# A decode-attention kernel: the output weights loaded once in long rows, in-place adds, and no Block

## The chip, the cores and the metric

One core of one Trainium2 chip. Times are device microseconds of one execution, quoted as the median of several. A profile also has a span, from the first to the last instruction of the profiled execution. In a profile PE is TensorE (its matmuls; PEld its weight loads), DVE is VectorE, ACT ScalarE, POOL GpSimd and SP SyncE; a packet is one record of the DMA in the trace, in these loads one contiguous row (64 loads of 128 rows of 32 KB have 8,192 packets of 32 KB). Executions of one kernel mostly agree within 0.3% (the kernel before: 662.87 to 664.14 us in four, 0.2%), so a difference of one or two microseconds in 663 is at the edge of what can be told.

## The reference

Attention of one new token against a cache, then a gated feed-forward layer, for a batch of 2:

```python
# B=2, D=512, 32 heads of Dh=128, cache length Sk=8192, F=1376, all bf16
q = (layernorm(x) @ wq)                       # per head
p = softmax(q . k_cache * Dh**-0.5)
o = p . v_cache                               # [B, 32*128]
h = x + o @ wo                                # wo: [4096, 512]
l = layernorm(h)
out = h + (relu(l @ W_gate) * (l @ W_up)) @ W_down
```

The two caches are 268 MB of the 281 MB that must be read. There is very little arithmetic per byte.

## The kernel before

A "pair" is two heads of one batch element; there are 32 pairs. The K and V of a pair are 128 rows of 32 KB each, one row in each SBUF partition, and four slots of 4 MB hold them:

```python
def kv(cache, p):
    hp, b = divmod(p, B)
    return cache[b, 2 * hp:2 * hp + 2].rearrange("h (p j) d -> (h p) (j d)", p=64)

with nc.Block() as block:
    @block.sync
    def _(eng):
        def load(s, cache, p):
            nc.sync.dma_start(slot[s][:], kv(cache, p)).then_inc(slot_sem[s], 16)
        def load_wo(dst, g, sem):      # two heads: 128 rows of 2 KB
            nc.sync.dma_start(
                dst[:], A_wo[2 * g * Dh:2 * (g + 1) * Dh].rearrange("(p r) n -> p (r n)", r=2)).then_inc(sem, 16)
        ...
        # cut: PE loop over two pairs: transposes and scores of K, collect, p.V, o_proj with wo_cur
        # cut: VectorE's share of the scores, for each pair p
        dve: prod = k_t[:, 0:jd, :] * q                     # L474
        cur, w, tog = prod[:, 0:jd, :], Dh, 0
        while w > 8:                                        # halving adds, L482
            half = w // 2
            o = tb[...] if tog == 0 else prod[:, 0:jd, 0:half]
            nc.vector.tensor_tensor(out=o, in0=cur[:, :, 0:half], in1=cur[:, :, half:w], op=ALU.add)
            cur, w, tog = o, half, tog ^ 1
        ...
        if p % 2 == 1 and 1 <= g < NI:
            load_wo(wo_cur, g, sem_wo)                      # every two pairs
        ...
        elif p == NP - 3:                                   # the last V, in two halves by columns
            for k, (j0, j1) in enumerate(((J // 2, J), (0, J // 2))):
                nc.sync.dma_start(slot[3][:, j0 * Dh:j1 * Dh],
                                  kv(A_v_cache, NP - 1)[:, j0 * Dh:j1 * Dh]).then_inc(sem_vl[k], 16)
```

`collect` sums the partial outputs of a pair of heads with 32 small float32 matmuls and `o_proj` multiplies the two finished heads by their rows of wo. After the last pair comes the tail: collection, projection, layer norm, the two up-projections, W_down, and the output.

The softmax here doesn't subtract the row's maximum and nothing guards it: scores larger than these inputs give would overflow.

Of the kernel before, what the change touches and what calls it, by code (L numbers as in the profile page):

```python
# [7 lines left out]
F32 = mybir.dt.float32  # L8
# [31 lines left out]
def bass_sequential_preLN__gqa_block_cached__glu_gated_reglu__decode_kernel(  # L40
# [26 lines left out]
    PG = 2  # L67
    NI = NP // 2 - 1
# [4 lines left out]
    with ExitStack() as es:  # L73
# [16 lines left out]
        sem_x, sem_wq, sem_wo, sem_wl, sem_out = S("x"), S("wq"), S("wo"), S("wl"), S("out")  # L90
# [5 lines left out]
        wo_cur = sb("wo_cur", [128, 2 * D], BF16)  # L96
# [3 lines left out]
        tb = sb("tb", [128, JC * 64], BF16)  # L100
# [9 lines left out]
        qrep = [tb[:, i * 512:(i + 1) * 512] for i in range(2)]  # L110
# [7 lines left out]
        NS = 4  # L118
        scores = [sb(f"scores{i}", [128, JC], F32) for i in range(NS)]
        e_t = [sb(f"e{i}", [128, J // VJ, 32], BF16) for i in range(PG)]  # L120
        zs = sb("zs", [128, 4, 2], F32)
        zr = sb("zr", [128, B], F32)
        zi = sb("zi", [128, B], F32)
        O_cur = sb("O_cur", [128, 2, B], BF16)
# [6 lines left out]
        h_r = sb("h_r", [128, 128], F32)  # L131
        o_r = sb("o_r", [128, 128], BF16)
# [5 lines left out]
        zero = sb("zero", [128, 8], BF16)  # L138
# [15 lines left out]
        with nc.Block() as block:  # L154

            @block.sync
            def _(eng):
# [4 lines left out]
                def load_wo(dst, g, sem):  # L162
                    nc.sync.dma_start(
                        dst[:], A_wo[2 * g * Dh:2 * (g + 1) * Dh].rearrange("(p r) n -> p (r n)", r=2)).then_inc(sem, 16)
# [5 lines left out]
                load_wo(wo_cur, 0, sem_wo)  # L170
                load_wo(wo_last, NI, sem_wl)
# [10 lines left out]
                for c in range(4):  # L182
                    pool.last()
                    pool.run(nc.gpsimd.tensor_copy(
                        out=sel[32 * c:32 * c + 32, :].rearrange("p (j a q) -> p j a q", j=VJ, q=PG),
                        in_=ident_f[32 * c:32 * c + 32, 32 * c:32 * c + 16].rearrange("p (q j a) -> p j a q", j=VJ, q=PG)))
# [3 lines left out]
                pool.run(nc.gpsimd.memset(zero[:], 0.0))  # L190
# [61 lines left out]
                dve.eng.memset(O_cur[:], 0.0).then_inc(d2p, 1)  # L252
                sp.wait(t_q)
                load(3, A_v_cache, 1)

# [25 lines left out]
                pe.wait(t_const, t_q2, t_q_b)  # L281
                pe.run(nc.tensor.matmul(Wp[:, 0:DC * B], lhsT=ident[:], rhs=zero[:], start=True, stop=False,
# [50 lines left out]
                def pv(T, p, parts):  # L333
# [4 lines left out]
                    for j0, j1, waits in parts:  # L338
                        for sem, val in waits:
                            nc.tensor.wait_ge(sem, val)  # L340
                        for j in range(j0, j1, VJ):
                            c = 32 * (n % 4)
                            i = nc.tensor.matmul(  # L343
                                Op[0][c:c + 32, :], lhsT=e_t[q][:, j // VJ, :],
                                rhs=v_t[:, j:j + VJ, :].rearrange("p j d -> p (j d)"),
                                start=(q == 0 and n < 4), stop=(q == PG - 1 and n >= J // VJ - 4))
                            n += 1
                    T.mark(("pv", p), i)

                def collect(T, a):  # L350
                    nc.tensor.wait_ge(a2p, a)
                    for r in range(2):
                        for jj in range(VJ):
                            for a_ in range(2):
                                i = nc.tensor.matmul(  # L355
                                    Ob[64 * a_:64 * a_ + 64, B * r:B * r + B],
                                    lhsT=os_sb[:].rearrange("p (j d r) -> p j r d", j=VJ, r=2)[:, jj, r, :],
                                    rhs=sel[:, (2 * jj + a_) * B:(2 * jj + a_) * B + B],
                                    start=(jj == 0), stop=(jj == VJ - 1))
                    T.mark("ob", i)  # L360

                def z_sum(T, bank):
                    for a in range(2):
                        i = nc.tensor.matmul(
                            bank[64 * a:64 * a + 64, ZC:ZC + 2 * B], lhsT=ones_f[:, 0:64],
                            rhs=zs[:].rearrange("p (b a) k -> p a b k", a=2)[:, a], start=True, stop=True)
                    T.mark("z", i)

                def o_proj(T, w, last=False):
                    wv = w[:].rearrange("p (r n c) -> p r c n", n=128, c=DC)  # L370
                    for r in range(2):
                        for c in range(DC):
                            i = nc.tensor.matmul(
                                Wp[:, c * B:(c + 1) * B], lhsT=wv[:, r, c, :], rhs=O_cur[:, r, :],
                                start=False, stop=last, skip_group_check=True)
                    T.mark("om", i)

                with nc.Fori(0, NI, engines=OrderedEngineSet([nc.tensor.engine])):
# [5 lines left out]
                    nc.tensor.wait_ge(d2p, 1)  # L384
                    nc.tensor.wait_ge(v2p, 2)
                    o_proj(body, wo_cur)
                    nc.tensor.sem_inc(d2p, -1)
                    pv(body, 1, ((jd, J, ((v2p, 3), (a2p, 12))), (0, jd, ((a2p, EV),))))
                    z_sum(body, Ob)
                    nc.tensor.sem_inc(g2p, -2)  # L390
                    nc.tensor.sem_inc(v2p, -3)
# [7 lines left out]
                k_part(tail, P0, 0, ((slot_sem[0], 256), (g2p, 1)))  # L399
                collect(tail, 6)  # L400
                ob_last_loop = tail.at["ob"]
                k_part(tail, P1, 7, ((slot_sem[2], 256), (g2p, 2)))
                nc.tensor.wait_ge(d2p, 1)
                nc.tensor.wait_ge(sem_wo, 16 * NI)
                o_proj(tail, wo_cur)
                pv(tail, P0, ((j30, J, ((slot_sem[1], 256), (a2p, 5))), (0, j30, ((a2p, 7),))))
                nc.tensor.wait_ge(a2p, 17)
                z_sum(tail, Op[1])
                pv(tail, P1, ((j31, J, ((sem_vl[0], 16), (a2p, 16))), (0, j31, ((sem_vl[1], 16), (a2p, 17)))))

# [25 lines left out]
                def normalize(bank, t_z):  # L436
                    dve.wait(t_z)
                    dve.run(nc.vector.tensor_reduce(  # L438
                        out=zr[:], in_=bank[:, ZC:ZC + 2 * B].rearrange("p (n k) -> p n k", k=2), axis=AX.X, op=ALU.add))
# [4 lines left out]
                def o_scale(t_ob):  # L444
                    dve.wait(t_ob)
                    nc.vector.tensor_tensor(
                        out=O_cur[:], in0=Ob[:, 0:2 * B].rearrange("p (r b) -> p r b", b=B),
                        in1=zi[:].unsqueeze(1).broadcast_to([128, 2, B]), op=ALU.mult).then_inc(d2p, 1)

                t_dm, t_s = {}, {}  # L450
                for p in range(NP):
# [12 lines left out]
                    if p < P0:  # L464
                        if p % 2 == 1:
                            nc.gpsimd.wait_ge(sem_wo, 16 * max(1, g))
                            nc.gpsimd.sem_inc(v2p, 1)
                        nc.gpsimd.wait_ge(slot_sem[s + 1], 16 * (g + 1))
                        nc.gpsimd.sem_inc(v2p, 1)

                    dve.wait((slot_sem[s], 16 * (g + 1)), t_q_b)
# [4 lines left out]
                    cur, w, tog = prod[:, 0:jd, :], Dh, 0  # L476
                    while w > 8:
                        half = w // 2
                        o = (tb[:, 0:jd * half].rearrange("p (j w) -> p j w", w=half) if tog == 0
                             else prod[:, 0:jd, 0:half])  # L480
                        dve.last()
                        dve.run(nc.vector.tensor_tensor(  # L482
                            out=o, in0=cur[:, :, 0:half], in1=cur[:, :, half:w], op=ALU.add))
                        cur, w, tog = o, half, tog ^ 1
                    dve.last()
                    sc = scores[p % NS]
                    t_s[p] = dve.run(nc.vector.tensor_reduce(out=sc[:, 0:jd], in_=cur, axis=AX.X, op=ALU.add))  # L487
                    if p % 2 == 0 and p >= 2:
                        t_ob = tok("ob", g) if g < NI else (pe.sem, ob_last_loop)
                        normalize(Ob, t_ob)  # L490
                        o_scale(t_ob)

                    for gg in range(ng):
                        act.wait(tokp("pt", p, gg))
                        if gg >= 2:
                            act.wait(tokp("sc", p, gg - 2))
                        elif p >= 1:
                            act.wait(tokp("sc", p - 1, NG - 2 + gg))
                        to_pe(nc.scalar.activation(  # L499
                            out=kT[gg % 2][:], in_=Tp[gg % 2][:].bitcast(BF16), func=ACT.Copy))  # L500
                    act.wait(tokp("sc", p, ng - 1), t_const)
                    exp(p, 0, lambda h, a: Sp[p % 2][h, 0:2 * ng * GT].rearrange(
                        "p (g j a) -> p g j a", a=2, j=VJ)[:, :, :, a])
                    if p % 2 == 0:
# [3 lines left out]
                    act.wait(t_s[p])  # L508
                    exp(p, 1, lambda h, a: sc[h, 0:jd].rearrange("p (g j) -> p g j", j=VJ))
# [4 lines left out]
                    if p % 2 == 1 and 1 <= g < NI:  # L514
                        sp.wait(tok("om", g))
                        load_wo(wo_cur, g, sem_wo)
# [11 lines left out]
                    elif p == NP - 2:  # L528
                        sp.wait(t_dm[p], tokp("pt", p, NG - 1))
                        for r0, r1 in ((0, 80), (80, 88), (88, FR)):  # L530
                            nc.sync.dma_start(
                                wd_last[r0:r1, :], B_W_down[F - FR + r0:F - FR + r1]).then_inc(sem_wd[3], 16)
# [148 lines left out]
```

## Time and profile before

| | before |
|---|---|
| time, median (range) of three executions | 663.05 us (662.87 to 664.14) |
| span of the profiled run | 661.1 us |
| bytes read, mean rate | 281 MB, 425 GB/s |
| third K load: last byte landed at | 64.7 us |
| last weight (W_down, third part): landed at | 657.8 us |

Landing times are the completion records that the trace has for each load: 16 of them for each of these loads, which I take as one from each DMA engine; "landed" means the last.

From the page of the kernel before: the span, the DMA rows of the 40 slices (busy tenths, and GB/s moved), the packet counts, the chain that ended last, and three groups of VectorE instructions.

```profile
span 661.1 us, 8515 instructions
...
DMA  9999999999999999999999999999999999999996
GB/s 381 429 426 439 421 438 429 434 424 430 438 430 428 428 430 440 427 431 428 428 438 430 428 430 430 437 427 428 429 434 432 432 424 432 436 419 442 430 419 276
DMA packets 12689, 281.22 MB, mean 425 GB/s; under 512 B 1442, under 2 KB 1540, under 8 KB 3972
...
DMA 71%; DVE 23%; PE 2%; POOL 2%; ACT 1%; issue 0%; SPq 0%; DVEq 0%; POOLq 0%
...
L474 DVE TENSOR_TENSOR prod<-slot,q_b 128x12288 bf16<-128x12288 bf16 (+1 forms) x32 | 207.7, 6491 | 128.9 <-DMA slot<-in_A_k_cache_dram 127.3
L482 DVE TENSOR_TENSOR tb<-prod 128x6144 bf16<-128x6144 bf16 (+1 forms) x64 | 136.8, 2137 | 2.2
L482 DVE TENSOR_TENSOR prod<-tb 128x3072 bf16<-128x3072 bf16 (+1 forms) x64 | 73.4, 1148 | 2.2
...
slot<-in_A_k_cache_dram SPq DMA_DIRECT2D x32, 4096.0 KB, 28.1
wo_cur<-in_A_wo_dram SPq DMA_DIRECT2D x15, 256.0 KB, 27.0
```

The DMA row is full in every slice but the last, and between the first slice and the last the rate never leaves 419 to 442 GB/s. A K load lands 28.1 us after it was issued, although 4 MB at this rate take 9.7 us: nearly three loads stand in the queue at all times. So nothing inside the loop but bytes and packets can move the time. The next view is the windows of the same kernel; the last two columns are the DMA's busy share and GB/s.

```profile
core 0: us, PE busy (x) PEld busy (x) DVE busy (x) ACT busy (x) POOL busy (x), PEclk, DMA share, GB/s
45.00:55.00 10.00, 3.17 (x22) 2.71 (x23) 9.93 (x3) 1.94 (x2) 6.51 (x1) 1.00 1.02 439
55.00:65.00 10.00, 6.38 (x73) 2.99 (x71) 4.44 (x5) 3.60 (x10) 0.22 (x1) 1.00 1.01 434
65.00:75.00 10.00, 3.40 (x29) 2.94 (x30) 9.93 (x3) 2.00 (x3) 6.29 (x1) 1.00 0.99 426
75.00:85.00 10.00, 7.18 (x88) 4.11 (x85) 5.44 (x8) 4.14 (x11) 0.96 (x1) 1.00 0.99 427
```

And the tail on PE, from the timeline of the same kernel: start, length, line, operands, count, and what ended the idle time before.

```profile
646.57 2.56 PE L343 MATMUL O<-slot,e 128*32 128x512 bf16 x32
649.84 1.13 PE L355 MATMUL Ob<-sel,os_sb 128*64 128x2 f32 x32 [0.71 <-ACT os_sb L547]
...
652.50 1.72 PE L584 MATMUL S<-d_b,slot 128*128 128x2 bf16 x44 [0.26 <-DVE d_b L564]
...
654.71 1.71 PE L584 MATMUL O<-d_b,slot 128*128 128x2 bf16 x44
```

The last half of V landed at 647.8 us. Its 16 matmuls, the collection (1.13 us), the projection and the up matmuls follow. Then the gate's 44 matmuls start at 654.71 us, because the gate weights landed at 654.66: the tail, too, waits for bytes.

### The profile page before, as it was taken

The numbers are of one execution on the slowest core, as the hardware profiler recorded it, in microseconds if no ns is written. First come the engines' busy times: TensorE is split into PE (matmuls) and PEld (weight loads), VectorE is DVE, ScalarE is ACT, GpSimd is POOL, SyncE is SP. The second block draws the span as 40 slices with busy tenths as digits, with TensorE's granted clock in tenths as the row PEclk, the third lists the DMA queues.
The fourth block names the chain that finished last, engine by engine and source line by source line (L and its number), as shares of the span: only waits on it lengthen the run. The fifth ranks groups of instructions, "written<-read, shape, count | busy, mean of one in ns | idle before, by whom it ended". The sixth has DMA issues, their size and how long they took to land.

```text
span 661.1 us, 8515 instructions
## 1 busy us (share of the span) xinstructions
PE 338.1 (51%) x3685; PEld 219.1 (33%) x3685; DVE 465.6 (70%) x274; ACT 198.3 (30%) x416; POOL 194.1 (29%) x48
## 2 busy tenths in 40 slices
PE   2635554446545445644536545445653536544767
PEld 2413432324333233432314333223432314333444
DVE  1766787767688676787767688676788767688681
ACT  0603332223332123332223332123332213332360
POOL 2021333332233331233332133332233332134000
PEclk9999966656555566555655555566555665556556
DMA  9999999999999999999999999999999999999996
GB/s 381 429 426 439 421 438 429 434 424 430 438 430 428 428 430 440 427 431 428 428 438 430 428 430 430 437 427 428 429 434 432 432 424 432 436 419 442 430 419 276
DMA packets 12689, 281.22 MB, mean 425 GB/s; under 512 B 1442, under 2 KB 1540, under 8 KB 3972
## 3 DMA queue, kind: packets, MB, share of 16 engines
q1 hardware_dynamic: 12664, 281.06, 99.3%
q8 instruction: 6, 0.10, 0.1%
q14 instruction: 7, 0.06, 0.0%
q10 hardware_dynamic: 12, 0.00, 0.0%
HBM read 281.05 MB, written 0.00 MB: 425 GB/s over the span
## 4 chain that ended last, share of the span: by engine, by line
DMA 71%; DVE 23%; PE 2%; POOL 2%; ACT 1%; issue 0%; SPq 0%; DVEq 0%; POOLq 0%
DMA slot<-in_A_k_cache_dram 64%; DVE prod L474 14%; DVE tb L482 6%; DMA slot<-in_B_W_gate_dram 4%; DVE prod L482 3%; POOL q2c L463 2%; DMA slot<-in_A_wq_dram 2%; PE T L325 1%; PE W L229 1%; ACT q_b L276 0%; PE O L271 0%; ACT kT L499 0%; PE O L584 0%; PE O L636 0%; PE S L313 0%
## 5 line engine op out<-in xcount | busy, mean ns | idle before, releaser
L463 POOL COPY q2c<-q 128x8 bf16<-128x8 bf16 x32 | 190.4, 5949 | 415.5 <-DMA slot<-in_A_k_cache_dram 384.2
L474 DVE TENSOR_TENSOR prod<-slot,q_b 128x12288 bf16<-128x12288 bf16 (+1 forms) x32 | 207.7, 6491 | 128.9 <-DMA slot<-in_A_k_cache_dram 127.3
L325 PE MATMUL T<-ident_f,slot 128*128 128x128 f32 x528 | 136.5, 426 | 219.8 <-POOL q2c L463 217.8
L499 ACT ACTIVATE kT<-T 128x1024 bf16<-128x1024 bf16 x132 | 131.4, 1022 | 388.9 <-PE T L325 385.0
L325 PEld LDWEIGHTS T<-ident_f,slot 128*128 128x128 f32 x528 | 98.3, 219 | 233.6 <-POOL q2c L463 231.4
L482 DVE TENSOR_TENSOR tb<-prod 128x6144 bf16<-128x6144 bf16 (+1 forms) x64 | 136.8, 2137 | 2.2
L343 PE MATMUL O<-slot,e 128*32 128x512 bf16 x1024 | 115.5, 615 | 18.7 <-ACT e L429 18.7
L482 DVE TENSOR_TENSOR prod<-tb 128x3072 bf16<-128x3072 bf16 (+1 forms) x64 | 73.4, 1148 | 2.2
L313 PE MATMUL S<-q2c,kT 128*128 128x4 bf16 x1056 | 50.3, 170 | 37.7 <-ACT kT L499 37.7
L313 PEld LDWEIGHTS S<-q2c,kT 128*128 128x128 bf16 x1056 | 44.0, 108 | 67.8 <-ACT kT L499 65.8
L343 PEld LDWEIGHTS O<-slot,e 128*32 128x32 bf16 x1024 | 32.4, 132 | 76.6 <-issue 53.8
L355 PE MATMUL Ob<-sel,os_sb 128*64 128x2 f32 x544 | 31.1, 245 | 26.2 <-ACT os_sb L507 25.5
L355 PEld LDWEIGHTS Ob<-sel,os_sb 128*64 128x64 f32 x544 | 29.7, 217 | 28.1 <-ACT os_sb L507 26.9
L487 DVE TENSOR_REDUCE scores<-prod 128x96 f32<-128x768 bf16 (+1 forms) x32 | 30.2, 945 | 1.1
L429 ACT ACTIVATE e<-scores 64x96 bf16<-64x96 f32 (+1 forms) x64 | 19.6, 307 | 22.8 <-DVE scores L487 22.1
L438 DVE TENSOR_REDUCE zr<-Ob 128x2 f32<-128x4 f32 x15 | 2.4, 162 | 28.1 <-PE Ob L355 28.1
L429 ACT ACTIVATE e<-S 64x32 bf16<-64x32 f32 (+1 forms) x64 | 13.0, 204 | 14.8 <-PE S L313 14.5
L429 ACT ACTIVATION_READ_ACCUMULATOR e<-S 64x1 f32 x64 | 12.9, 201 | 0.7
L429 ACT ACTIVATION_READ_ACCUMULATOR e<-scores 64x1 f32 x64 | 11.8, 184 | 0.0
L507 ACT ACTIVATE os_sb<-O 128x512 f32<-128x512 f32 x16 | 9.6, 597 | 0.4
L276 ACT ACTIVATE q_b<-O 128x512 bf16<-128x512 f32 x8 | 4.3, 595 | 16.9 <-PE O L271 16.9
L234 DVE CAST qT<-W 128x64 bf16<-128x64 f32 x1 | 0.2, 224 | 11.2 <-PE W L229 11.2
(74 smaller groups left out, 72.0 us busy)
## 6 DMA issues: line engine op xcount, KB each, us to landing
slot<-in_A_k_cache_dram SPq DMA_DIRECT2D x32, 4096.0 KB, 28.1
slot<-in_A_v_cache_dram SPq DMA_DIRECT2D x31, 4096.0 KB, 31.3
slot<-in_A_wq_dram SPq DMA_DIRECT2D x1, 4096.0 KB, 12.3
slot<-in_A_v_cache_dram SPq DMA_DIRECT2D x2, 2048.0 KB, 29.6
wo_cur<-in_A_wo_dram SPq DMA_DIRECT2D x15, 256.0 KB, 27.0
slot<-in_B_W_up_dram SPq DMA_DIRECT2D x1, 1376.0 KB, 26.2
slot<-in_B_W_gate_dram SPq DMA_DIRECT2D x1, 1376.0 KB, 29.1
slot<-in_B_W_down_dram SPq DMA_DIRECT2D x2, 512.0 KB, 30.3
```

Source lines behind the costliest of these rows:

```text
L229: i = nc.tensor.matmul(Wp[:, h * B:(h + 1) * B], lhsT=wq[:, c, h * Dh:(h + 1) * Dh], rhs=lT[:, c * B:(c + 1) * B], start=(c == 0), stop=(c ...
L313: i = nc.tensor.matmul(Sp[p % 2][:, 2 * jj:2 * jj + 4], lhsT=kv_[:, k, r, :], rhs=q2c[p % 2][:, r, :], start=(r == 0), stop=(r == 1))
L325: i = nc.tensor.transpose(Tp[g % 2][:, k * 128:(k + 1) * 128], k_t[:, j:j + 2, :].rearrange("p j d -> p (j d)").bitcast(F32), ident_f[:])
L343: i = nc.tensor.matmul(Op[0][c:c + 32, :], lhsT=e_t[q][:, j // VJ, :], rhs=v_t[:, j:j + VJ, :].rearrange("p j d -> p (j d)"), start=(q == ...
L355: i = nc.tensor.matmul(Ob[64 * a_:64 * a_ + 64, B * r:B * r + B], lhsT=os_sb[:].rearrange("p (j d r) -> p j r d", j=VJ, r=2)[:, jj, r, :], ...
L429: i = nc.scalar.activation(out=e_t[q][h, j0 // VJ:j1 // VJ, 8 * q:8 * q + 8].rearrange("p g (j a) -> p g j a", a=2)[:, :, :, a], in_=src(h ...
L463: nc.gpsimd.tensor_copy(out=q2c[p % 2][:], in_=q2[:, p]).then_inc(g2p, 1)
L474: t_dm[p] = dve.run(nc.vector.tensor_tensor(out=prod[:, 0:jd, :], in0=k_t[:, 0:jd, :], in1=qv, op=ALU.mult))
L482: dve.run(nc.vector.tensor_tensor(out=o, in0=cur[:, :, 0:half], in1=cur[:, :, half:w], op=ALU.add))
L487: t_s[p] = dve.run(nc.vector.tensor_reduce(out=sc[:, 0:jd], in_=cur, axis=AX.X, op=ALU.add))
L499: to_pe(nc.scalar.activation(out=kT[gg % 2][:], in_=Tp[gg % 2][:].bitcast(BF16), func=ACT.Copy))
L507: to_pe(nc.scalar.activation(out=os_sb[:], in_=Op[0][:], func=ACT.Copy))
```

## The change

The intent: the 15 loads of wo in 2 KB rows become one early load of 30 heads in 32 KB rows, issued as two DMAs of 112 and 8 rows, and one projection of all of them near the end; VectorE's halving adds write over their input, which frees the buffer that the big tile needs; the program stands in the main block. The core of the diff:

```diff
+    DR = 32
+    KP = (H - 2) * Dh // DR                      # 120 rows
-        wo_cur = sb("wo_cur", [128, 2 * D], BF16)
-        tb = sb("tb", [128, JC * 64], BF16)
+        X = sb("X", [KP, DR * D], BF16)
-        with nc.Block() as block:
-            @block.sync
-            def _(eng):
+        if True:
+            def program():
+                wo_rows = A_wo[0:KP * DR].rearrange("(p r) n -> p (r n)", r=DR)
                 load(3, A_v_cache, 1)
+                nc.sync.dma_start(X[0:112, :], wo_rows[0:112]).then_inc(sem_wo[0], 16)
+                nc.sync.dma_start(X[112:KP, :], wo_rows[112:KP]).then_inc(sem_wo[1], 16)
 # collect: 32 matmuls of 64 columns become 4 of 128
-                    for r in range(2):
-                        for jj in range(VJ):
-                            for a_ in range(2):
-                                i = nc.tensor.matmul(Ob[64 * a_:64 * a_ + 64, B * r:B * r + B], ...)
+                    for jj in range(VJ):
+                        i = nc.tensor.matmul(Ob[:, 0:4], lhsT=os_sb[:, jj * Dh:(jj + 1) * Dh], ...)
 # loop: o_proj becomes o_gather (2 matmuls that put the head into its place in O_all)
-                    o_proj(body, wo_cur)
+                    o_gather(body)
 # tail: one projection of 30 heads between the last two K
+                for r in range(DR):
+                    i = nc.tensor.matmul(
+                        Op[1][32 * (r % 4):32 * (r % 4) + B, :], lhsT=O_all[0:KP, r, :], rhs=X[:, r * D:(r + 1) * D],
+                        start=(r < 4), stop=(r >= DR - 4))
 # VectorE adds
-                        o = (tb[:, 0:jd * half]... if tog == 0 else prod[:, 0:jd, 0:half])
                         dve.run(nc.vector.tensor_tensor(
-                            out=o, in0=cur[:, :, 0:half], in1=cur[:, :, half:w], op=ALU.add))
+                            out=prod[:, 0:jd, 0:half], in0=prod[:, 0:jd, 0:half], in1=prod[:, 0:jd, half:w], op=ALU.add))
 # ScalarE in the tail: copies of the last K before the exponentials of the pair before it
+                        evacs()
+                        exp_dve(P0, j30)
+                        exp_pe()
+                        exp_dve(P1, j31)
-                    if p % 2 == 1 and 1 <= g < NI:
-                        load_wo(wo_cur, g, sem_wo)
```

Cut: the odd rows of W_down load at the start and not at the end, and the probability tile is 16 columns wide and not 32.

## The prediction

> **What bounds the kernel now.** The DMA engines. The page's DMA row reads 9 in all slices but the last; the windows view gives a DMA share of 1.00 and 428 to 433 GB/s from 20 to 620 us. VectorE is busy 70%, PE 51%. The chain of waits is 71% DMA; its VectorE pieces (the product, 14%) only say when the next K load was issued, and that is early: a K load lands 28.1 us after issue, while 4 MB take 9.8 us, so nearly three loads are queued. Two pairs take 39.53 us (K landings), 17.04 MB at 431 GB/s.[...] After the last weight lands (657.8 us) come 8 matmuls, one VectorE op, the output DMA (1.9 us) and a closing barrier.
>
> **What the change does, costed.**
> 1. wo: same bytes, other packets. A 2 KB packet takes 84 ns in the trace, a 32 KB packet 1218 ns. Fifteen loads are 120 packets an engine, about 9.6 us at an 80 ns pitch, 0.66 us in every two pairs. The new load is 120 rows of 32 KB: 7 packets (8.5 us) on each engine for 112 rows; the other 8 rows run on 8 engines only[...], which then spend 9.7 us. Eight engines save 1.1 us, eight nothing; the last byte comes from the later ones. Estimate: 0 to 0.8 us, 0.3 likely. Two pairs shorten to about 38.9 us; the 8.5 to 9.7 us are paid once, before the third K lands (near 74 us instead of 64.7).
> 2. No Block: the entry branch (about 0.05 us) and the closing drain and barrier (660.72 to 661.06 us, 0.35 us) go, all on the chain.
> 3. In-place adds: the old adds already mix contiguous and 256-byte-pitch rows at about 0.55 ns an element; I expect the same times (3.4, 1.8, 1.0, 0.6 us). VectorE has 5 us of slack per 19.8 us pair: nothing gained.
> 4. PE: the collection, 32 matmuls and 1.9 us per two pairs, becomes 4; e is half as wide; 8 projection matmuls become 2 gathers. All hidden. In the tail come 32 projection matmuls of 512 columns (estimated 3.6 us, from the 32 probability matmuls of like width) and two ScalarE copies. They fit before the last V half (647.8 us), as ScalarE now copies the last K before the earlier pair's exponentials. The last collection is 0.7 us shorter, but the gate weights (654.7 us) and W_down (657.8 us) then decide.
> 5. W_down's odd rows load early: bytes unmoved.
>
> **Sum.** 0.3 + 0.05 + 0.35 + about 0.1 = 0.8 us: predicted 662.2 us, 8 in 10 between 661.2 and 663.3. Faster by over 2%: 1%; within 2%: 97%; slower: 2%.
>
> **What would show it.** DMA share 1.00; two-pair period near 38.9 us; third K landing near 74 us; about 1,900 fewer packets under 8 KB; last weight landing 0 to 1.2 us earlier; span ends with the output's landing, no barrier; the adds' mean times unchanged; collection time down several-fold; the gate's matmuls still released by DMA.
>
> **What would make it wrong.** In-place adds at half rate: 7 us more per pair, and VectorE would bound the loop. The tail projection delaying the last V's matmuls beyond 649 us. The 8-row part leaving eight engines so late that the last byte comes later than now. Instruction fetches (16 KB packets of 1.05 us, three after 631 us) falling on the latest engine.

(Two passages are cut from it, where marked, since no trace shows them: an upper limit of the DMA rate, and the ground on which it put the 8 rows on eight engines. No term of the sum is cut: 0.3 + 0.05 + 0.35 + about 0.1 us make the 0.8 us. The eight engines themselves fit the trace of the changed kernel: the load of the 8 rows has one completion record at 18.1 us, half a microsecond after its issue, and then eight, from 70.7 to 76.3 us, where the 112-row load has sixteen; and the packets under 512 B, which the completions are among, number 1210 with it and 1202 in the run without it.)

## The result

| | before | changed |
|---|---|---|
| time, median (range) of four executions | 663.0 us (662.87 to 664.14) | 674.19 us (672.24 to 675.06) |
| span of the profiled run | 661.1 us | 673.8 us |
| third K landed at | 64.7 us | 85.7 us |
| two pairs take (mean of the loop) | 39.48 us | 38.85 us |
| last weight landed at | 657.8 us | 669.5 us |

The ratio is 1.0161, with a 95% interval of 1.0136 to 1.0186. A ratio here is the mean time of one kernel's runs over the mean time of the other's of the same rounds, so it isn't quite the ratio of the medians. The change was meant to save under a microsecond and costs 11.

The lines of the changed kernel's page that answer to those of before:

```profile
span 673.8 us, 7501 instructions
...
DMA  9999999999999999999999999999999999999995
GB/s 374 424 436 263 315 434 428 434 430 431 432 430 434 432 430 436 430 430 430 432 434 430 428 432 434 434 430 430 432 433 430 432 432 436 430 430 432 434 415 225
DMA packets 10786, 281.22 MB, mean 417 GB/s; under 512 B 1210, under 2 KB 1564, under 8 KB 1948
...
DMA 71%; DVE 24%; PE 2%; POOL 1%; SPq 0%; ACT 0%; issue 0%; DVEq 0%; POOLq 0%
...
L498 DVE TENSOR_TENSOR prod<-slot,q_b 128x12288 bf16<-128x12288 bf16 (+1 forms) x32 | 207.7, 6492 | 132.2 <-DMA slot<-in_A_k_cache_dram 130.6
L504 DVE TENSOR_TENSOR prod<-prod 128x6144 bf16<-128x6144 bf16 (+4 forms) x128 | 210.2, 1642 | 4.4
...
slot<-in_A_k_cache_dram SPq DMA_DIRECT2D x32, 4096.0 KB, 27.4
X<-in_A_wo_dram SPq DMA_DIRECT2D x1, 3584.0 KB, 56.0
```

The busy row of the DMA still reads 9 everywhere, and this is the trap: a slow packet counts as busy for as long as it takes, so that the windows below show a busy share of 0.94 at 184 GB/s. The GB/s row tells it. Two slices, the fourth and fifth, moved 263 and 315 GB/s; the others, but for the first and the last, lie at 415 to 436. The windows of the changed kernel at that place, with the same columns:

```profile
core 0: us, PE busy (x) PEld busy (x) DVE busy (x) ACT busy (x) POOL busy (x), PEclk, DMA share, GB/s
45.00:55.00 10.00, 3.22 (x23) 2.76 (x24) 9.93 (x3) 1.94 (x2) 6.47 (x1) 1.00 1.10 400
55.00:65.00 10.00, 6.15 (x65) 2.64 (x63) 4.07 (x4) 3.60 (x10) 0.00 (x0) 1.00 0.98 242
65.00:75.00 10.00, 0.00 (x0) 0.00 (x0) 0.00 (x0) 0.00 (x0) 0.00 (x0) 0.56 0.94 184
75.00:85.00 10.00, 0.00 (x0) 0.00 (x0) 0.00 (x0) 0.00 (x0) 0.00 (x0) 0.50 1.01 433
```

From the second V's end at 53 to 56 us until 76 us, while the new load of wo runs, the DMA engines move 184 to 242 GB/s. In the packet records, the median 32 KB packet takes 1.22 us in this kernel and in the kernel before, and outside this stretch 42 of some 8,100 take over 1.3 us; of the 189 that start from 51 to 76 us, 158 do, half of these 2.3 us or more, the longest 3.7 us. Compute stands still from 65 to 85 us, but that only follows from the missing data.

How the 12.2 us between the two profiled runs (675.06 against 662.86 us) divide, from the traces:

- The third K lands 21.1 us later (85.73 against 64.66 us): the second V, which is in front of wo, is held up by 1.8 us (56.34 against 54.59), wo takes 19.9 us behind it (to 76.27), and the third K follows 9.5 us after that, where before it took 10.1 us. Over the 14 two-pair periods that follow, the changed kernel gains 8.8 us back (0.63 us in each, since the small loads of wo are gone), and 0.6 us more with the last weights. Left over at the last weight: 669.48 less 657.79, 11.7 us.
- From the last weight to the end of the span: 4.28 us against 3.27 us, so 1.0 us more.
- Outside the span (time of the execution less its span): 1.31 us against 1.80 us, so 0.5 us less.

The tail on PE, from the changed kernel's timeline:

```profile
659.79 1.89 PE L357 MATMUL O<-slot,e 128*16 128x512 bf16 x16 [0.74 <-DMA slot<-in_A_v_cache_dram]
662.37 1.87 PE L367 MATMUL Ob<-sel,os_sb 128*128 128x4 f32 x8 [0.70 <-ACT os_sb L588]
...
665.78 1.73 PE L633 MATMUL S<-d_b,slot 128*128 128x2 bf16 x44 [0.26 <-DVE d_b L613]
...
667.79 1.71 PE L633 MATMUL O<-d_b,slot 128*128 128x2 bf16 x44
```

The gate weights landed at 666.4 us, but the gate's matmuls start at 667.79 us, straight behind PE's own work. The collection takes 1.87 us, not 1.13. The granted clock goes with it (section "The tail" has the test): in the kernel before a full-clock stretch of 3.4 us fell on 647.9 to 651.3 us, just after the last V; in the changed kernel the last one was 643.1 to 653.3 us, and everything after it ran at half clock (0.50 granted). In the clock records of both traces every full-clock stretch after the one at the start (to 88 us before, to 66 us in the changed kernel) lasts 3.4 us, but for this last one of 10.2 us. What sets the clock isn't shown.

### The profile page after: what moved, and what is told of

The parts are those of the page before. It is cut to its first block, busy times and chain, and to the rows that moved or that the text cites. A ratio compares the mean times of both kernels' runs of the same rounds, so it can differ in the third digit from the quotient of the medians.

```text
span 673.8 us, 7501 instructions
## 1 busy us (share of the span) xinstructions
PE 341.6 (51%) x3190; PEld 216.2 (32%) x3190; DVE 468.8 (70%) x306; ACT 198.8 (30%) x418; POOL 192.4 (29%) x48
## 2 busy tenths in 40 slices
DMA packets 10786, 281.22 MB, mean 417 GB/s; under 512 B 1210, under 2 KB 1564, under 8 KB 1948
## 4 chain that ended last, share of the span: by engine, by line
DMA 71%; DVE 24%; PE 2%; POOL 1%; SPq 0%; ACT 0%; issue 0%; DVEq 0%; POOLq 0%
DMA slot<-in_A_k_cache_dram 66%; DVE prod L498 14%; DVE prod L504 10%; DMA slot<-in_A_v_cache_dram 5%; POOL q2c L488 1%; PE O L357 1%; PE T L339 0%; PE Ob L367 0%; PE S L633 0%; PE O L633 0%; PE O L685 0%; ACT kT L520 0%; DVE scores L509 0%; SPq L166 0%; ACT e L444 0%
## 5 line engine op out<-in xcount | busy, mean ns | idle before, releaser
L339 PE MATMUL T<-ident_f,slot 128*128 128x128 f32 x528 | 133.6, 419 | 228.0 <-POOL q2c L488 228.0
L504 DVE TENSOR_TENSOR prod<-prod 128x6144 bf16<-128x6144 bf16 (+4 forms) x128 | 210.2, 1642 | 4.4
L339 PEld LDWEIGHTS T<-ident_f,slot 128*128 128x128 f32 x528 | 96.7, 216 | 243.1 <-POOL q2c L488 242.2
L357 PE MATMUL O<-slot,e 128*16 128x512 bf16 x1024 | 115.7, 617 | 22.5 <-ACT e L444 21.8
L357 PEld LDWEIGHTS O<-slot,e 128*16 128x16 bf16 x1024 | 28.8, 118 | 83.6 <-issue 59.1
L367 PE MATMUL Ob<-sel,os_sb 128*128 128x4 f32 x136 | 31.8, 357 | 24.9 <-ACT os_sb L535 24.2
L367 PEld LDWEIGHTS Ob<-sel,os_sb 128*128 128x128 f32 x136 | 30.3, 327 | 27.2 <-ACT os_sb L535 25.6
L453 DVE TENSOR_REDUCE zr<-Ob 128x4 f32<-128x8 f32 x15 | 2.5, 167 | 34.0 <-PE Ob L367 34.0
L444 ACT ACTIVATE e<-scores 64x96 bf16<-64x96 f32 (+1 forms) x64 | 19.5, 304 | 19.8 <-DVE scores L509 19.0
L373 PEld LDWEIGHTS Ob<-zs,ones_f 128*128 128x128 f32 x30 | 6.4, 268 | 12.0 <-issue 12.0
```

What stands on the lines that cost most here:

```text
L339: i = nc.tensor.transpose(Tp[g % 2][:, k * 128:(k + 1) * 128], k_t[:, j:j + 2, :].rearrange("p j d -> p (j d)").bitcast(F32), ident_f[:])
L357: i = nc.tensor.matmul(Op[0][c:c + 16, :], lhsT=e_t[q][:, j // VJ, :], rhs=v_t[:, j:j + VJ, :].rearrange("p j d -> p (j d)"), start=(q == ...
L367: i = nc.tensor.matmul(Ob[:, 0:4], lhsT=os_sb[:, jj * Dh:(jj + 1) * Dh], rhs=sel[:, 4 * jj:4 * jj + 4], start=(jj == 0), stop=(jj == VJ - 1))
L373: T.mark("z", nc.tensor.matmul(bank[:, ZC:ZC + 8], lhsT=ones_f[:], rhs=zs[:], start=True, stop=True))
L444: i = nc.scalar.activation(out=e_t[q][h, j0 // VJ:j1 // VJ, 8 * q:8 * q + 8].rearrange("p g (j a) -> p g j a", a=2)[:, :, :, a], in_=src(h ...
L504: dve.run(nc.vector.tensor_tensor(out=prod[:, 0:jd, 0:half], in0=prod[:, 0:jd, 0:half], in1=prod[:, 0:jd, half:w], op=ALU.add))
```

## The experiments

**The theory.** A load that is cut by partitions, so that each DMA writes fewer than 128 of them, is slower for it, although the bytes and the source are the same. The reason that I had in mind is a mechanism that no trace or run of this case shows; it is cut, here and in the expectations, where marked. What is left of the theory there is, up to the eight pieces of 16 partitions, the expectation that has no other name. Its packet times, 2.4 us for 64 rows and up to 4.9 us for 16, were estimates of mine from the 1.22 us of a 32 KB packet and from that reason. **Rivals:** wo's rows are slow to read wherever they go; only the 8-row part, on 8 engines, does the harm; or the rest of the change (tail, clock) does.

### wo as 128 rows

```diff
-        X = sb("X", [KP, DR * D], BF16)
+        X = sb("X", [128, DR * D], BF16)
-                nc.sync.dma_start(X[0:112, :], wo_rows[0:112]).then_inc(sem_wo[0], 16)
-                nc.sync.dma_start(X[112:KP, :], wo_rows[112:KP]).then_inc(sem_wo[1], 16)
+                nc.sync.dma_start(X[:], A_wo.rearrange("(p r) n -> p (r n)", r=DR)).then_inc(sem_wo[0], 16)
```

> The changed kernel, with wo loaded whole as 128 rows of 32 KB in one DMA in place of 112 rows and 8 rows (8 rows more than needed, 256 KB, 0.6 us). [...] all 16 engines spend 9.7 us on it, no 32 KB packet takes much over 1.3 us, the third K lands at 74 to 76 us instead of 85.7, time 662 to 664 us. Rival, the source (wo's rows in HBM are slow to read in 32 KB pieces whatever their number): packets of 2 to 3.7 us stay, third K near 86 us, time near 674 us. Rival, the rest of the change (tail projection, clock): time stays above 670 us though the third K lands early.

Measured: correct, 663.7 us (662.34 to 663.91) against 662.93 us of before on the same chip; ratio 1.0005, interval 0.9991 to 1.0019. The third K landed at 74.0 us, and the load of wo took 9.7 us. The windows of this run:

```profile
45.00:55.00 10.00, 3.17 (x22) 2.72 (x23) 9.93 (x3) 1.94 (x2) 6.51 (x1) 1.00 1.05 452
55.00:65.00 10.00, 5.29 (x65) 2.30 (x63) 4.11 (x4) 3.49 (x10) 0.00 (x0) 0.83 0.99 424
```

One DMA in place of two, with 256 KB more to read, takes the whole loss away. The source, the 32 KB rows, the place in the program, the tail projection and the in-place adds are the same as in the changed kernel, so none of them costs the 11 us. Only the cutting by partitions does.

### The same cutting in the kernel before

In the kernel before, only the second V load was cut, same bytes to the same places:

```diff
-                load(3, A_v_cache, 1)
+                nc.sync.dma_start(slot[3][0:112, :], kv(A_v_cache, 1)[0:112]).then_inc(sem_vx[0], 16)
+                nc.sync.dma_start(slot[3][112:128, :], kv(A_v_cache, 1)[112:128]).then_inc(slot_sem[3], 16)
```

(GpSimd, which tells PE that this V is there, waits for the extra semaphore too.)

> The kernel before; only the second V load (pair 1, issued at 16.7 us) is cut by partitions into 112 and 16 rows, same bytes to the same places. [...] packets of 2 us and more appear, the third K's last landing moves from 64.7 us to 70 to 76 us and stays that late, time 668 to 675 us. Source theory (wo's rows are slow): nothing moves, 663 us. Imbalance theory (only the 8 rows on 8 engines hurt): 16 rows give one to each engine, nothing moves.

Measured: 674.96 us (674.11 to 675.32), ratio 1.0175. The third K landed at 76.9 us (64.7 before), a little later than I had written. Two windows:

```profile
45.00:55.00 10.00, 1.90 (x8) 1.57 (x8) 8.52 (x2) 0.74 (x1) 6.58 (x1) 1.00 0.99 242
55.00:65.00 10.00, 3.54 (x49) 2.87 (x48) 5.62 (x5) 4.79 (x12) 0.00 (x0) 1.00 0.93 180
```

With the cache as source and nothing else changed, one load of 64 cut this way costs 12 us. So neither wo as source nor the rest of the change is needed, and imbalance isn't needed either: here the small part gives each engine one row (the cut adds 16 packets under 512 B, 1458 against 1442, which I take as a completion from each engine).

### Two halves of 64 partitions, and a control

```diff
+                nc.sync.dma_start(slot[3][0:64, :], kv(A_v_cache, 1)[0:64]).then_inc(sem_vx[0], 16)
+                nc.sync.dma_start(slot[3][64:128, :], kv(A_v_cache, 1)[64:128]).then_inc(slot_sem[3], 16)
```

> The kernel before; the same V load cut into partitions 0 to 63 and 64 to 127. Every engine still gets 4 rows of each half[...]. [...] 32 KB packets of about 2.4 us, the load takes 19.4 us instead of 9.7, the third K lands near 74 us, time near 672 us. Source or imbalance theory: third K at 64.7 us, time 663 us.

Measured: 675.7 us (674.27 to 676.69), ratio 1.0186; third K at 77.7 us. Both are nearly 4 us more than I had written. The load itself took the expected time, 19.8 us (48.41 to 68.23 us), but the second K, the load in front of it, landed at 48.4 us in place of 44.9: a load that is still landing when the cut one begins is held up as well. Of the packets in the stretch that took longer than usual, half took over 2.55 us, about twice 1.22; 24 took over 2.7 us, up to 3.5, all of them starting before 47 us.

The control reads the same two halves one after the other, but writes each over all 128 partitions in 16 KB rows:

```diff
+                nc.sync.dma_start(slot[3][:, 0:SLOT//2],
+                    kv(A_v_cache, 1)[0:64].rearrange("p (t n) -> (p t) n", t=2)).then_inc(sem_vx[0], 16)
+                nc.sync.dma_start(slot[3][:, SLOT//2:SLOT],
+                    kv(A_v_cache, 1)[64:128].rearrange("p (t n) -> (p t) n", t=2)).then_inc(slot_sem[3], 16)
```

> Control of the last run: the same two halves of the source, in the same order and on the same engines count, but each half is written over all 128 partitions in 16 KB rows (the rows of this one V pair then stand in the wrong places: a wrong result on purpose). [...] no loss, third K lands near 64.7 us, time 663 us. If reading one half of the source at a time is what costs, the loss of the 64-row run stays, near 672 us.

Measured: 663.06 us (662.99 to 663.09), ratio 1.0000; third K at 64.3 us. (The output still passed the comparison; one pair's misplaced V rows are within its tolerance, so this isn't evidence that the kernel is right.) The windows of the two runs, first the halves on 64 partitions, then the control:

```profile
45.00:55.00 10.00, 0.00 (x0) 0.00 (x0) 6.56 (x1) 0.00 (x0) 6.54 (x1) 1.00 1.01 203
55.00:65.00 10.00, 5.44 (x56) 4.44 (x56) 7.58 (x5) 5.54 (x12) 0.04 (x1) 1.00 1.00 210
```

```profile
45.00:55.00 10.00, 3.23 (x24) 2.77 (x25) 9.93 (x3) 1.94 (x2) 6.45 (x1) 1.00 1.04 446
55.00:65.00 10.00, 6.32 (x73) 2.92 (x71) 4.69 (x5) 3.60 (x10) 0.53 (x1) 1.00 1.02 437
```

Both runs cut the load in two and read the same addresses in the same order. 64 partitions as the destination give 203 to 210 GB/s, 128 give 437 to 446. So it is the destination that counts, and neither the number of DMAs nor the source.

### Eight pieces of 16 partitions

The same load once more, now in eight DMAs (`slot[3][0:16]`, `[16:32]`, and so on). This tells "the fewer neighbouring partitions, the slower" from "anything under 128 rows runs at half rate".

> The kernel before with the second V load cut into eight DMAs of 16 partitions: each engine has one row of each[...]. [...] 32 KB packets up to 4.9 us, dozens over 4 us (the 64-row run had none over 2.7 us), a slower load than in the 64-row run[...]: third K between 70 and 90 us, time 670 to 690 us. Rival, a DMA of fewer than 128 rows simply runs at half rate: packets of 2.4 to 2.7 us as with 64 rows, time near 675 us.

Measured: 690.13 us (688.32 to 692.18), ratio 1.0403; third K at 92.5 us, both just outside of what I had written, on the slow side. 116 packets took over 4 us; the slow ones have a median of 4.41 us. (The "none over 2.7 us" of my expectation is a slip: the 64-row run had the 24 named above.)

```profile
45.00:55.00 10.00, 0.00 (x0) 0.00 (x0) 5.98 (x1) 0.00 (x0) 5.95 (x1) 1.00 1.01 118
55.00:65.00 10.00, 5.43 (x56) 4.44 (x56) 8.17 (x6) 5.54 (x12) 0.62 (x1) 1.00 1.20 141
```

The eight pieces of 512 KB landed 3.7 to 4.5 us apart, 4.2 us on average, which is 125 GB/s. This is the rate of the eight in a row: the completions of one piece lay up to 6.2 us apart, so neighbouring pieces overlapped. For DMAs of 16, 64 and 128 neighbouring partitions the rates were about 125, 203 to 210, and 431 GB/s. The half-rate rival falls, and so does a rate that is simply proportional to the partitions. (The DMA share above 1 in these windows is packets that are counted where they start.)

### Without the 8 rows

```diff
-                nc.sync.dma_start(X[112:KP, :], wo_rows[112:KP]).then_inc(sem_wo[1], 16)
-                        ... lhsT=O_all[0:KP, r, :], rhs=X[:, r * D:(r + 1) * D] ...
+                        ... lhsT=O_all[0:112, r, :], rhs=X[0:112, r * D:(r + 1) * D] ...
```

> The changed kernel without its 8-row DMA (8 rows of wo missing, a wrong result on purpose). If the 112-row part alone makes nearly all of the loss: the third K still lands after 80 us, time 670 to 673 us. If the 8 rows on 8 engines[...] do most of it: third K near 75 us, time 663 to 666 us.

Measured: 669.22 us (667.81 to 669.77), ratio 1.0085; third K at 82.0 us. It lies between the two sizes that I had written. The 112-row part alone costs about 6 us over the kernel before; the 8 rows, one fourteenth as many bytes, cost another 5 us (674.19 less 669.22; the runs are from different chips). In the two traces the last weight lands 4.4 us later with the 8 rows (669.48 against 665.07); the rest is the tail, which had more of the full clock without them (see "The tail"). Eight packets of 1.2 us on 8 of 16 engines (eight completions, as said beside the prediction) would be 1.2 us. That much is there: from then on the 16 completions of a K load lie 4.1 us apart, against 2.8 us without the 8 rows and 2.2 us in the kernel before. The rest is slow packets: with the 8 rows each of the 29 packets of 32 KB that start from 65 to 70 us takes 2.2 us or more, up to 3.7; without them none takes over 2.7 us.

### Only the Block taken away

```diff
-        with nc.Block() as block:
-            @block.sync
-            def _(eng):
+        if True:
+            def program():
```

> The kernel before with only the Block taken away. If the closing barrier is all it costs: the span ends within 0.1 us of the output's landing, the first DMA is issued at 0.74 us as before (the changed kernel's was), and the time falls by 0.3 to 0.4 us, to about 662.6 us. If the place of the program also matters for instruction fetches, the last weight's landing moves by half a microsecond or more from 657.8 us.

Measured: 661.97 us against 663.01 us of before; ratio 0.9991, interval 0.9977 to 1.0005. The span is 0.5 us shorter: the output's landing ends it, as expected (0.35 us), and the last weight lands 0.13 us earlier. The other half microsecond isn't in the span at all: an execution takes 1.3 us more than its span without the Block (1.27 to 1.34 in five runs) and 1.8 us with it (1.76 to 1.90 in nine). The first DMA is issued at 0.74 us in both, so the entry branch cost nothing that can be seen. The five runs fall into two groups, three near 661.9 and two near 663.1 us.

### The tail

What the 128-row run kept of the loss is in the tail. Its last weight landed at 658.3 us and its span ended 4.3 us later, as in the changed kernel. Two edits of that run tried it. The first brings the old order back on ScalarE:

```diff
                     else:
+                        exp_dve(P0, j30)
                         evacs()
-                        exp_dve(P0, j30)
                         exp_pe()
                         exp_dve(P1, j31)
```

(with the counts that PE waits for changed to match).

> The run with wo as 128 rows, with the old order on ScalarE in the tail (the earlier pair's exponentials before the copies of the last K). Theory: the tail after the last V half runs at half clock because the new order spends the full-clock stretch earlier; with the old order the full-clock slice should fall in the last 16 us again, the collection after the last V should take 1.1 us and not 1.9, and the time should fall by about 1 us, to 662.5 us. Rival: the new projection itself delays the tail, and with the old order on top the last V's matmuls start later than its landing: 663.5 to 665 us.

Measured: 664.48 us (664.15 to 666.41), ratio 1.0025: slower. Two lines of its timeline show both halves of the expectation at work:

```profile
651.02 2.82 PE L356 MATMUL O<-slot,e 128*16 128x512 bf16 x32
...
654.55 1.05 PE L366 MATMUL Ob<-sel,os_sb 128*128 128x4 f32 x8 [0.71 <-ACT os_sb L587]
```

The collection takes 1.05 us, at full clock, as the theory had it. (This profile is of the slowest of the five executions, 666.41 us.) But the last V's matmuls start at 651.02 us, 2.7 us after its landing (648.4 us), since the pair before was not done. So the new ScalarE order is needed for the new projection to fit, as the prediction said; the place of the full clock is a second thing.

What the clock is worth shows in the run without the 8 rows. Its tail is the changed kernel's but for those rows, and its last full-clock stretch fell on 656.9 to 660.3 us, after the last V (655.3 us):

```profile
657.83 1.05 PE L366 MATMUL Ob<-sel,os_sb 128*128 128x4 f32 x8 [0.71 <-ACT os_sb L587]
...
662.05 0.41 PE L643 MATMUL T<-ident,hb 128*2 128x32 bf16 x16
662.40 1.72 PE L632 MATMUL O<-d_b,slot 128*128 128x2 bf16 x44
```

The collection takes 1.05 us and not 1.87, the gate's matmuls start 0.4 us after the gate's landing (661.96 us) and not 1.4, and the span ends 3.3 us after the last weight and not 4.3. So the lost microsecond of the tail goes with the clock.

The second cuts the last V in three quarters and one quarter, so that less follows its last landing:

```diff
-  enumerate(((J // 2, J), (0, J // 2)))
+  enumerate(((J // 4, J), (0, J // 4)))
-  pv(tail, P1, ((j31, J, ((sem_vl[0], 16),)), (0, j31, ((sem_vl[1], 16),))))
+  pv(tail, P1, ((J // 4, J, ((sem_vl[0], 16),)), (0, J // 4, ((sem_vl[1], 16),))))
```

> The run with wo as 128 rows, with the last V cut in three quarters and one quarter in place of halves, so that 8 matmuls and not 16 follow its last landing. If the tail's chain starts from that landing, as the trace of the 128-row run shows: 0.7 to 0.9 us less, about 662.9 us (half clock) and the gate's matmuls closer to the gate's landing. If the weights' landings bind: no change.

Measured: 662.64 us (662.42 to 663.0) against 663.01 us of before, ratio 0.9993, and 1.1 us under the 128-row run (on another chip). In its trace the gate's matmuls start at 655.28 us, 0.04 us after the gate's landing: the tail waits for bytes again. Part of this is luck of the clock: here the collection ran at full clock (1.05 us).

### A version that beats both

The kernel before, in the main block, with the last V cut in three quarters and one quarter; wo stays in its small loads.

> A candidate to beat both: the kernel before, in the main block (its time was 661.97 us, with single runs near 661.9 or near 663.1), and the last V cut in three quarters and one quarter. If the slower runs are those in which the half clock makes the tail's chain from the last V outlast the gate's landing, the shorter chain takes them away: all runs near 661.9 us, median 661.6 to 662.2 us. If those runs come from the DMA side: two groups as before.

Measured: correct, 662.09 us (661.87 to 662.37) against 663.04 us (662.78 to 664.02); ratio 0.9984, interval 0.9970 to 0.9998. It is one microsecond faster than the kernel before and twelve faster than the changed one. The slower group of the run without Block is not seen in these five runs. That the cut of V adds anything to leaving out the Block isn't shown: three of the five runs without Block alone took 661.84 to 661.97 us. In the tail PE now has time to spare before the gate's landing:

```profile
647.80 0.62 PE L342 MATMUL O<-slot,e 128*32 128x512 bf16 x8 [0.24 <-DMA slot<-in_A_v_cache_dram]
649.12 1.13 PE L354 MATMUL Ob<-sel,os_sb 128*64 128x2 f32 x32 [0.70 <-ACT os_sb L546]
...
654.71 0.46 PE L583 MATMUL O<-d_b,slot 128*128 128x2 bf16 x9 [0.86 <-DMA slot<-in_B_W_gate_dram]
```

(The last line is cut by the window.) PE idles 0.86 us for the gate.

## Why the prediction was wrong

The predicted time was 662.2 us, 661.2 to 663.3; measured were 674.19 us. Point by point:

- **What bounds the kernel: right.** DMA before and after; the loop's periods fell from 39.48 to 38.85 us, "about 38.9".
- **The step that failed is point 1, in the words "7 packets (8.5 us) on each engine for 112 rows" and "8 engines only ..., which then spend 9.7 us".** It counted packets for each engine and took the packet's time, 1218 ns, from loads over 128 partitions. It asked how many engines a DMA gets and not where they write. In the load half of the slow packets took 2.3 us or more, wo took 19.9 us, and the third K was held back by 21.1 us, not 8.5 to 9.7. The 128-row run shows what the sum is worth without the fault: third K at 74.0 us, the predicted "near 74". The prediction named "the 8-row part leaving eight engines so late" as a risk; that part was 4 to 5 us, of which the unevenness that the prediction meant is about 1.3 us (9.7 less 8.5 is 1.2), and the 112-row part, not suspected, 6 us.
- **The gain itself was as small as estimated.** With the cutting mended the last weight still lands no earlier: in the 128-row run at 658.34 us, 0.55 us after that of before. One completion does this: the fifteen others come by 657.08 us there, and by 657.55 us before, although this run reads 256 KB more (0.6 us at 431 GB/s). In all three tails that I looked at, 16 KB instruction fetches of about 1.1 us fall between the weights; that they make the late one is not shown.
- **No Block: right in direction, too small.** 0.35 us of barrier as said, and half a microsecond more outside the span. The 0.05 us of the entry branch weren't there.
- **In-place adds: right.** 210.2 us in 128 instructions, 1642 ns each; before 136.8 and 73.4 us in 128 instructions, the same sum.
- **The collection: wrong.** "32 matmuls ... become 4" was read as a saving. Before, it was 31.1 us busy in the whole run; after, 31.8 us, in a quarter of the instructions. Being hidden in the loop it cost nothing there, but "the last collection is 0.7 us shorter" turned into 0.7 us longer, at half clock.
- **The tail: the projection fits, right** (3.58 us against an estimate of 3.6), and the last V's matmuls started 0.05 us after its landing. **"The gate's matmuls still released by DMA": wrong**: PE was 1.4 us late for them, 1 us of it with the half clock (0.4 us in the run without the 8 rows, whose collection had the full clock). This is 1 us of the 11.

What stays open: why nearly every packet is slow while the 112 rows load. The run of the 112 rows alone lost some 8 us at the third K (82.0 us, against 74.0 with 128 rows), and in its trace all 88 packets of 32 KB that start from 56.5 to 68 us take over 1.3 us. The trace doesn't name the engine of a packet, so how 112 rows are dealt out, and whether a slow packet holds up those of other engines, can't be told from these runs. That the cutting by partitions is the cause is shown, and so is that a load ran slower with fewer neighbouring partitions written at a time (about 125 GB/s with 16, 203 to 210 with 64, 236 to 242 with 112 in the windows from 55 to 65 us, 431 with 128). Why it is so is not shown: no run tested a reason, and 32 partitions, or 64 that are not neighbours, were not run.

## What to carry to other kernels

Cut a big load by columns and not by partitions, so that each part still writes all 128 of them: two halves of 64 partitions ran at 203 to 210 GB/s, two over all 128 at 437 to 446. The load in front of the cut one was held up too (the second K landed at 48.4 us in place of 44.9), and rounding 120 rows up to 128 was worth 10 us, although it reads more. When counting DMA time by packets, take a packet's time from a DMA of the same partition shape (32 KB took 1.22 us over 128 partitions; the median of the slow ones was 2.55 us over 64 and 4.41 us over 16), and judge a full DMA by GB/s in short windows, since slow packets count as busy (share 0.94 at 184 GB/s). In a kernel that is bound by bytes, look for the rest at the two ends: the closing barrier and the piece of work that follows the last landing.
